# Filter steps, in-place sums and small stores moved in the first phase of a long convolution with a gate; ScalarE's long jobs of the last phase put into separate rows

## The chip, the cores and the metric

The kernel runs on one core of a Trainium2 chip. The metric is the device time of one execution in microseconds. TensorE is the matrix engine (PE in the profile), VectorE is DVE, ScalarE is ACT, GpSimd is POOL, and SyncE (SP) only issues transfers. Three of the engines issue transfers in this kernel: SyncE, ScalarE and GpSimd, each from its own queue, in which a transfer stands among the engine's other work and waits in line.

## The reference, cut to what matters

All arrays are float32 on entry, batch 4, sequence 12800, width 128.

```python
h_mlp = np.maximum(pos_emb @ w1, 0.0) @ w2          # the filter, made from pos_emb
h_filt = h_mlp * np.exp(-0.01 * pos)[:, None]
u = x * v
y = irfft(rfft(u, n=2*S) * rfft(h_filt, n=2*S)[None], n=2*S)[:, :S]
x = x * y                                            # the long convolution, gated by x
gate_pre[t] = sum over k < 5 of conv_w[k] * x[t - 4 + k]
out = (sigmoid(gate_pre) * (x @ w_val)) @ w_out
```

## The kernel before, in words

The sequence of 12800 is cut into J = 2 halves of 6400, and each half into N1 = 100 by N2 = 64. The transforms are matrix products over n1 (100) and n2 (64).

**First phase** (`signal` and `filt`). For each of the 64 n2 a tile of x and v is loaded by three transfers on SyncE (64, 32 and 4 partitions, L298). VectorE forms the product x*v in the tile's first half (`product`, L315). Two n2 form a pair, n2 and its mirror: `prep` forms their sum and difference in the tiles' second halves (L326, L327), and from these, for each n2, two sums us and ud (L334) in tiles of their own, two buffers each. TensorE multiplies us and ud with the table fsd into fp (L379, two matmuls for each of c = 0, 1), ScalarE copies fp to st (L380, two copies to one n2), and the spectrum part st is stored to the scratch tensor a_u in three transfers: 64 and 32 partitions from ScalarE's queue (L386), 4 partitions from SyncE's queue one n2 later (`flush`, L397). st has four buffers. The tiles for x and v come from a ring: four general buffers ld 0 to 3 and two own ones xv6, xv7, and from the time when the filter's input is used up also ld 4 and 5 (until the 48th load). A pair of tiles goes back to the ring after the second n2's us and ud are formed (`release`), and the next loads into them are issued there (`fetch`).

The filter is made beside it, in three parts that share the engines with the signal: 32 steps that transpose pos_emb and apply w1 (L228 to L242), 32 steps of the transform over n1 (L256 to L262, copied out by ScalarE), and 26 steps (one to begin with and 25 of four k1 each) of twiddle and transform over n2 (`turned`, L269 to L282: four ScalarE and four VectorE operations, eight matmul passes and a ScalarE copy). The two are written as generators. A list of costs gives each filter step a price, and after each half of an n2 as many filter steps are recorded as keep the spent cost in step with the signal's progress; the factor FS = 0.87 makes the filter end at about n2 = 56. By that list the three parts take 18.4, 20.7 and 16.5 n2. The order in which the code records the operations is the order of each engine's queue (`manual_schedule`); no scheduler moves anything there.

Six tables (dft, tw, inv and the three int64 weight arrays) are loaded from ScalarE's queue at n2 = 8 and 12. Near the end GpSimd issues the first loads of the second phase (rows of a_u that are complete); the rest of these rows come from SyncE.

**Second phase** (`filter_pair`, `spectrum`, `times`, `inverse`): pairs of k1, not touched.

**Last phase** (from L547): 32 groups of R = 4 rows; every row passes through y_sum (TensorE, sd), y_copy (ScalarE, sd_sb L602), y_trans two rows later (TensorE transposes tp L609, ScalarE dif L611), y_join (VectorE yr L619 and L620, GpSimd product into ext L622), five taps of the short convolution for a whole group (tap 0 on ScalarE, gt L634; taps 1 to 4 on VectorE, one in each row, L637), a sigmoid for a whole group (ScalarE, sg L641), the value product (TensorE, v_ps L646), the gated product (VectorE, gd L651), the projection (TensorE, o_ps L656) and a copy and store (ScalarE, o_sb L664). ext holds 16 rows and 4 rows of halo in front; every fourth group begins a new ext, and `fill_halo` copies the last four rows of the one before (L588), or parts of the tail rows at the start of a half (L583 to L586), and for the last ext of a half also the tail rows (L590). In the loop, tap 0 of the next group, the sigmoid and the halo copy all stand in row 3 of the four. In what follows rows are counted r = 0 to 3 as in the loop, and a row's operations stand in each engine's queue in the order in which the loop writes them.

Of the kernel before, what the change touches and what calls it, by code (L numbers as in the profile page):

```python
# [9 lines left out]
F32 = mybir.dt.float32  # L10
# [13 lines left out]
B, S, D, FO, KC = 4, 12800, 128, 64, 5  # L24
J, N1, N2 = 2, 100, 64
# [4 lines left out]
R = 4  # L30
# [88 lines left out]
def tile_longconv_gate(  # L119
# [20 lines left out]
    nc = tc.nc  # L140
# [41 lines left out]
    BD = B * D  # L182
# [23 lines left out]
    with tc.tile_pool(name="p1", bufs=1) as p1, tc.tile_pool(name="ps1", bufs=1, space=PSUM) as ps1:  # L206
# [77 lines left out]
                yield  # L284

        ring = list(enumerate(LD[0:4]))
        ring += [(6, p1.tile([128, 4 * BD], F32, name="xv6")), (7, p1.tile([128, 4 * BD], F32, name="xv7"))]
        for i, (_, t) in enumerate(ring):
            (nc.vector, nc.gpsimd)[i in (2, 5)].memset(t, 0.0)
        ahead, fetched = [], [0]  # L290
        BACK = 48

# [8 lines left out]
                    free_at[i] = n - 2 * N2  # L301
                fetched[0] += 1

        def release():
            for i, t, _ in pair:
                if i not in (4, 5) or fetched[0] < BACK:
                    ring.append((i, t))
            pair.clear()

        def halves(t):  # L310
            return t.rearrange("p (w h e) -> p w h e", w=2, h=2)

# [2 lines left out]
            nc.vector.tensor_tensor(u[:, 0], u[:, 0], u[:, 1], op=ALU.mult)  # L315
            pair.append((*it, u))

        pair = []

        def prep(n):  # L320
            if n == 0:
                product(ahead.pop(0))
            if n % 2 == 0:
                product(ahead.pop(0))
                a, b = (u for _, _, u in pair)
                nc.vector.tensor_tensor(a[:, 1], a[:, 0], b[:, 0], op=ALU.add)  # L326
                nc.vector.tensor_tensor(b[:, 1], a[:, 0], b[:, 0], op=ALU.subtract)  # L327
                srcs = a, b
            else:
                srcs = pair[1][2], pair[0][2]  # L330
            out = []
            for c, op in enumerate((ALU.add, ALU.subtract)):
                w = p1.tile([128, BD], F32, name="us" if c == 0 else "ud", bufs=US)
                nc.vector.tensor_tensor(w, srcs[c][:, 1, 0], srcs[c][:, 1, 1], op=op)  # L334
                out.append(w)
            if n % 2 == 1:
                release()
                fetch()
                if n + 1 < N2:
                    product(ahead.pop(0))  # L340
            return out

        US = 2

        def signal():
            fetch(4)
            load_pos(0)
            fetch()
            load_pos(HC)
            ready = [prep(0)]  # L350
            for n in range(N2):
                if n == 8:
                    nc.scalar.dma_start(out=dft, in_=t_dft)
                    nc.scalar.dma_start(out=tw, in_=t_tw)
                    nc.scalar.dma_start(out=inv, in_=t_inv)
                if n == 12:
                    for dst, src in ((wval, w_val), (wout, w_out), (cw, conv_w.rearrange("k d -> d k"))):
                        raw = p1.tile(list(dst.shape), mybir.dt.int64, name=f"raw{len(raws)}")
                        nc.scalar.dma_start(out=raw, in_=src)
                        raws.append((dst, raw))  # L360
                if n in (18, 22, 26):
                    _narrow(nc, p1, *raws[n // 4 - 4])
                if n == BACK + 2:
                    load_w(0)
                if n == N2 - 3:
                    for part in EARLY:
                        load_a(0, part, nc.gpsimd)
                if n == N2 - 1:
                    for part in EARLY:
                        load_a(1, part, nc.gpsimd)  # L370
                if n + 1 < N2:
                    ready.append(prep(n + 1))
                both = ready.pop(0)
                st = p1.tile([128, 2, J * BD], F32, name="st", bufs=4)
                for c in range(2):
                    fp = ps1.tile([128, J, BD], F32, name="fp", bufs=2)
                    for j in range(J):
                        h = slice(j * 64, j * 64 + 64)
                        nc.tensor.matmul(out=fp[:, j], lhsT=fsd[h, c], rhs=both[c][h], start=True, stop=True)  # L379
                    nc.scalar.copy(out=st[:, c], in_=fp.rearrange("k j e -> k (j e)"))  # L380
                    yield
                src = st.rearrange("k c e -> k (c e)")
                row = n % 2 * N2 + n // 2 * 2
                dst = a_u[:, row:row + 2].rearrange("k c e -> k (c e)")
                for k0, k, step, p0 in PARTS[:2]:
                    nc.scalar.dma_start(out=dst[k0:k0 + k], in_=src[p0:p0 + step * (k - 1) + 1:step])  # L386
                rest.append((dst, src))
                if len(rest) > 1 or n + 1 == N2:
                    flush()
# [3 lines left out]
        def flush():  # L393
            while len(rest) > 1 or rest and n_done[0]:
                dst, src = rest.pop(0)
                k0, k, step, p0 = PARTS[2]
                nc.sync.dma_start(out=dst[k0:k0 + k], in_=src[p0:p0 + step * (k - 1) + 1:step])  # L397

        n_done = [False]

        FS = 0.87
        with tc.manual_schedule():
            sig, fil = signal(), filt()
            n_sig = 2 * N2
            cost = [0.7, 0.9] * (J * N2 // 8) + [0.9] * (FO // 2) + [0.4] + [0.9] * (N1 // 4)
            spent, steps = 0.0, iter(cost)
            for i in range(n_sig):
                next(sig, None)
                while spent < sum(cost) and spent * n_sig * FS <= (i + 1) * sum(cost):
                    next(fil, None)  # L410
                    spent += next(steps, sum(cost))
            for _ in sig:
                pass
            n_done[0] = True
            flush()
            for _ in fil:
                pass
# [126 lines left out]
    with tc.tile_pool(name="p3", bufs=1) as p3, tc.tile_pool(name="ps3", bufs=1, space=PSUM) as ps3:  # L544
# [3 lines left out]
        EG = 4  # L548
# [27 lines left out]
        def fill_halo(j, q):  # L576
            e = exts[j, q]
            if q == 0:
                t, m = tails[j], N1 // 2
                if j == 0:  # L580
                    nc.vector.memset(e[:, 0:HALO, :, 0:1], 0.0)
                else:
                    nc.scalar.copy(out=e[:, 0:HALO, :, 0:1], in_=tails[j - 1][:, :, :, m + 1:m + 2])  # L583
                nc.scalar.copy(out=e[:, 0:HALO, :, 1:m + 1], in_=t[:, :, :, 0:m])
                nc.scalar.copy(out=e[:, 0:HALO, :, m + 1:N1 - 1], in_=t[:, :, :, m + 2:N1])  # L585
                nc.scalar.copy(out=e[:, 0:HALO, :, N1 - 1:N1], in_=t[:, :, :, m:m + 1])  # L586
            else:
                nc.scalar.copy(out=e[:, 0:HALO], in_=exts[j, q - 1][:, EG * R:])  # L588
            if q == NG // EG - 1:
                nc.scalar.copy(out=e[:, EG * R:], in_=tails[j])  # L590

        def y_sum(s, r):
            sd = ps3.tile([128, B * D], F32, name="sd", bufs=2)
# [76 lines left out]


        AHEAD3, NT, LAG = 3, len(groups), 2
        y_run, gd_last, o_last = [], None, None
        with tc.manual_schedule():
            for s in range(3):
                load_rows(s, (2,))
# [5 lines left out]
            for t in range(-AHEAD3, NT + 2):  # L682
# [9 lines left out]
                for r in range(R):  # L692
                    done = y_run.pop(0) if len(y_run) == LAG or s >= NT and y_run else None
                    if done:
                        y_trans(*done)
                    v_ps = value(t - 1, r) if 0 <= t - 1 < NT else None
                    if o_last is not None:
                        finish(*o_last)
                        o_last = None
                    if gd_last is not None:  # L700
                        o_last = gd_last[0], gd_last[1], project(gd_last[2])
                        gd_last = None
                    if s < NT and r % 2 == 0:
                        y_sum(s, r)
                        y_sum(s, r + 1)
                    if 0 <= t < NT:
                        tap(t, r + 1)
                    if r == R - 1 and 0 <= t + 1 < NT:
                        tap(t + 1, 0)
                    if v_ps is not None:  # L710
                        gd_last = t - 1, r, gated(t - 1, r, v_ps)
                    if done:
                        y_join(*done)
                    if s < NT:
                        y_copy(s, r)
# [46 lines left out]
```

## Time and profile before

| | |
|---|---|
| median of 3 runs | 1182.41 us (1181.82 to 1184.42) |
| the profiled execution's own time | 1177.74 us, of which its span 1176.0 us |
| mean granted TensorE clock | 0.953 |
| busy over the span: TensorE, VectorE, ScalarE, GpSimd | 1027.8, 992.6, 622.6, 679.7 us |
| moved by DMA | 329.98 MB, mean 281 GB/s |
| stretch 340 to 380 us | end of the first phase; ScalarE's last copy into st at 378 us |
| stretch 400 to 760 us | second phase |
| stretch 811 to 1135 us | last phase, full rows |

In a row of the timeline stand the start and the length in us, the engine, the line, the operation with the tile that it writes and those that it reads, and in brackets how long the engine stood idle before it and on what. An engine's name with a q (ACTq, SPq) is its queue issuing a transfer. In the table of windows each engine's busy time stands with its count of instructions. Waits are inferred from semaphores: where several were waited for, the last one is named, and an engine that is kept at its own transfer issue is shown as waiting for some transfer.

### The profile page before, as it was taken

The numbers are of one execution on the slowest core, as the hardware profiler recorded it, in microseconds if no ns is written. First come the engines' busy times: TensorE is split into PE (matmuls) and PEld (weight loads), VectorE is DVE, ScalarE is ACT, GpSimd is POOL, SyncE is SP. The second block draws the span as 40 slices with busy tenths as digits, with TensorE's granted clock in tenths as the row PEclk, the third lists the DMA queues.
The fourth block names the chain that finished last, engine by engine and source line by source line (L and its number), as shares of the span: only waits on it lengthen the run. The fifth ranks groups of instructions, "written<-read, shape, count | busy, mean of one in ns | idle before, by whom it ended". The sixth has DMA issues, their size and how long they took to land. (4 is left out here: it accounts for less than half of the span.)

```text
span 1176.0 us, 19204 instructions
## 1 busy us (share of the span) xinstructions
PE 1027.8 (87%) x6968; PEld 479.7 (41%) x6968; DVE 992.6 (84%) x1146; ACT 622.6 (53%) x1000; POOL 679.7 (58%) x290
## 2 busy tenths in 40 slices
PE   3767788967675799999999999988999999999986
PEld 1333345534341344444444444333444444444432
DVE  6678886659986799999999999718999999999996
ACT  1233366667774244444444444346676767676763
POOL 1000000000000699999999999928889898898880
PEclk9789889888989799999999999999999999999999
DMA  8889898875879789989999989787787777687622
GB/s 253 289 312 321 287 336 323 310 254 203 307 277 323 260 300 307 311 305 311 309 311 310 314 307 306 245 284 291 272 304 260 282 276 295 263 312 259 236 85 112
DMA packets 81384, 329.98 MB, mean 281 GB/s; under 512 B 11812, under 2 KB 13036, under 8 KB 62092
## 3 DMA queue, kind: packets, MB, share of 16 engines
q1 hardware_dynamic: 38512, 196.90, 50.1%
q10 hardware_dynamic: 42204, 130.02, 28.0%
q0 software_dynamic: 576, 1.84, 0.6%
q8 instruction: 57, 0.93, 0.3%
q14 instruction: 35, 0.29, 0.1%
HBM read 197.64 MB, written 131.07 MB: 280 GB/s over the span
## 5 line engine op out<-in xcount | busy, mean ns | idle before, releaser
L622 POOL TENSOR_TENSOR ext<-yr,xr 128x400 f32<-128x400 f32 x120 | 303.2, 2528 | 40.5 <-DVE yr L620 38.3
L637 DVE SCALAR_TENSOR_TENSOR gt<-ext,cw,gt 128x1600 f32<-128x1600 f32 x128 | 240.7, 1881 | 0.8 <-ACT gt L634 0.8
L380 ACT COPY st<-fp 128x1024 f32<-128x1024 f32 x128 | 128.7, 1027 | 174.9 <-PE fp L379 66.7
L484 ACT COPY c_sb<-c_ps 128x1024 f32<-128x1024 f32 x100 | 101.4, 1014 | 201.7 <-PE c_ps L479 194.8
L479 PE MATMUL c_ps<-va,ld 64*64 64x512 f32 x1600 | 194.1, 594 | 0.0
L468 DVE TENSOR_TENSOR va<-z_ps,h_sb 128x2048 f32<-128x2048 f32 x50 | 114.6, 2291 | 49.7 <-ACT h_sb L452 32.9
L513 POOL TENSOR_TENSOR va<-va,vb 128x1024 f32<-128x1024 f32 x50 | 118.6, 2373 | 45.6 <-DVE vb L468 45.5
L198 POOL DMA_DIRECT2D ld<-a_u x4 | 2.7, 683 | 240.6 <-DMA a_u<-st 240.6
L379 PE MATMUL fp<-us,fsd 64*128 64x512 f32 x256 | 87.2, 763 | 62.3 <-ACT st L380 35.5
L656 PE MATMUL o_ps<-gd,wout 128*128 128x400 f32 x256 | 112.4, 521 | 19.2 <-DVE gd L651 11.2
L595 PE MATMUL sd<-ld,inv 128*64 128x512 f32 x512 | 124.8, 605 | 2.0 <-ACT sd_sb L602 1.0
L522 POOL TENSOR_TENSOR va<-va,vb 128x1024 f32<-128x1024 f32 x50 | 119.6, 2392 | 0.0
L521 POOL TENSOR_TENSOR vc<-vc,vd 128x1024 f32<-128x1024 f32 x50 | 119.0, 2379 | 0.0
L462 PE MATMUL z_ps<-ld,ld 64*64 64x512 f32 x800 | 111.3, 606 | 7.4 <-DMA a_u<-st 4.0
L479 PEld LDWEIGHTS c_ps<-va,ld 64*64 64x64 f32 x1600 | 73.7, 135 | 101.2 <-issue 100.9
L602 ACT COPY sd_sb<-sd 128x512 f32<-128x512 f32 x128 | 76.1, 595 | 72.2 <-PE sd L595 55.5
L468 DVE TENSOR_TENSOR vb<-z_ps,h_sb 128x2048 f32<-128x2048 f32 x50 | 114.0, 2280 | 0.0
L646 PE MATMUL v_ps<-ext,wval 128*128 128x400 f32 x256 | 107.1, 500 | 0.0
L479 PE MATMUL c_ps<-vc,ld 64*64 64x512 f32 x800 | 98.2, 604 | 3.6 <-ACT c_sb L484 3.6
L609 PEld LDWEIGHTS tp<-ident,sd_sb 128*128 128x128 f32 x512 | 58.3, 140 | 75.8 <-PE sd L595 49.5
L609 PE MATMUL tp<-ident,sd_sb 128*128 128x128 f32 x512 | 79.9, 280 | 3.7 <-DVE yr L620 2.6
L619 DVE TENSOR_TENSOR yr<-tp,dif 128x204 f32<-128x204 f32 x128 | 45.9, 358 | 42.0 <-ACT dif L611 40.8
(85 smaller groups left out, 1560.6 us busy)
## 6 DMA issues: line engine op xcount, KB each, us to landing
c_y<-c_sb ACTq DMA_DIRECT2D x100, 512.0 KB
ld<-a_u SPq DMA_DIRECT2D x48, 1024.0 KB
a_u<-st ACTq DMA_DIRECT2D x64, 512.0 KB
ld<-c_y SPq DMA_DIRECT2D x64, 512.0 KB
xr<-in_xt_dram SPq DMA_DIRECT2D x32, 800.0 KB
out_dram<-o_sb ACTq DMA_DIRECT2D x32, 800.0 KB
ld<-in_xv_dram SPq DMA_DIRECT2D x46, 512.0 KB
a_u<-st ACTq DMA_DIRECT2D x64, 256.0 KB
```

The costliest lines, as they stand in the source:

```text
L380: nc.scalar.copy(out=st[:, c], in_=fp.rearrange("k j e -> k (j e)"))
L462: nc.tensor.matmul(out=z[half[h], c], lhsT=wk[half[c], 0, half[h]], rhs=a2[half[c], h, j], start=True, stop=True)
L468: nc.vector.tensor_tensor(out, z.rearrange("p (b d) -> p b d", d=D).unsqueeze(1).to_broadcast([128, n, B, D]), h_sb.unsqueeze(2).to_broadc ...
L479: nc.tensor.matmul(out=c_ps[half[m], h], lhsT=wk[half[h], 1 + c, half[m]], rhs=vt[half[h], c].rearrange("p b d -> p (b d)"), start=(i == 0 ...
L513: nc.gpsimd.tensor_tensor(va[:, 0:2], va[:, 0:2], vb[:, 0:2], op=ALU.add)
L521: nc.gpsimd.tensor_tensor(vc, vc, vd, op=ALU.add)
L522: nc.gpsimd.tensor_tensor(va[:, 2:4], va[:, 2:4], vb[:, 2:4], op=ALU.add)
L595: nc.tensor.matmul(out=sd[c * N2:(c + 1) * N2], lhsT=inv[:, c], rhs=rows_in[s, c][:, r * B * D:(r + 1) * B * D], start=True, stop=True)
L609: nc.tensor.transpose(out=tp[:, b], in_=t[:, b], identity=ident)
L622: nc.gpsimd.tensor_tensor(e[:, r0 + r], yr, xr, op=ALU.mult)
L637: nc.vector.scalar_tensor_tensor(gt, rows(t, k), cw[:, k:k + 1], gt, op0=ALU.mult, op1=ALU.add)
L656: nc.tensor.matmul(out=o_ps, lhsT=wout, rhs=gd, start=True, stop=True)
```

## The change: what it does

In the first phase:

- us and ud lose their tiles. The sums are written into the first half of the pair's tiles, whose products are no longer needed then. A tile of x and v is therefore given back later: after the second n2's matmuls instead of after its sums.
- The ring has one tile more (xv8): seven, and nine when ld 4 and 5 join it.
- The list of costs is gone. The filter's parts are spread evenly over n2 = 2 to 17 (32 steps), 17 to 35 (32) and 35 to 62 (26).
- The 4-partition stores of st and the six table loads are issued from GpSimd instead of SyncE and ScalarE; one more of the starting memsets is GpSimd's.

In the last phase the halo copy moves from row 3 to row 0 of the next group, tap 0 of the next group from row 3 to row 1, the copy of the tail rows to row 2; the sigmoid stays in row 3.

SyncE's queue in the first phase before; ld_74 to ld_77 are ring tiles, the L397 rows the small stores of st, two n2 each time:

```order
L397 DMA a_u<-st 4x2048 x2
L298 DMA ld_74<-in_xv_dram 64x2048
L298 DMA ld_74<-in_xv_dram 32x2048
L298 DMA ld_74<-in_xv_dram 4x2048
L298 DMA ld_75<-in_xv_dram 64x2048
L298 DMA ld_75<-in_xv_dram 32x2048
L298 DMA ld_75<-in_xv_dram 4x2048
L397 DMA a_u<-st 4x2048 x2
```

and GpSimd's queue now, from the last starting memset's successor on (a_u<-st are the same small stores, raw the int64 weights, ld_78 and ld_79 the filter's input buffers, cleared before they join the ring):

```order
L398 DMA a_u<-st 4x2048 x7
L352 DMA dft<-in_tab_dft_dram 128x256
L353 DMA tw<-in_tab_tw_dram 128x200
L354 DMA inv<-in_tab_inv_dram 128x128
L398 DMA a_u<-st 4x2048 x4
L358 DMA raw_523<-in_moe_w_val_dram 128x128
L358 DMA raw_525<-in_moe_w_out_dram 128x128
L358 DMA raw_527<-in_moe_conv_w_dram 128x5x1
L398 DMA a_u<-st 4x2048 x5
L248 MEMSET ld_78 128x2048
L248 MEMSET ld_79 128x2048
L398 DMA a_u<-st 4x2048 x44
```

The small stores stand no longer between the loads on SyncE, but behind each other on GpSimd, with the tables and two memsets between them.

ScalarE's queue in the last phase before, at the row in which a new ext has begun (dif, o_sb and sd_sb are each row's own copies):

```order
L611 COPY dif<-tp_6325 128x204
L664 COPY o_sb<-o_ps 128x400
L634 ACTIVATE gt<-ext,cw 128x1600
L602 COPY sd_sb<-sd 128x512
L641 ACTIVATE sg<-gt 128x1600
L588 COPY ext<-ext 128x1600
L611 COPY dif<-tp_6359 128x204
L664 COPY o_sb<-o_ps 128x400
L602 COPY sd_sb<-sd 128x512
```

and now, from the halo copy of row 0 to row 3's first copies:

```order
L587 COPY ext<-ext 128x1600
L608 COPY dif<-tp_6260 128x204
L661 COPY o_sb<-o_ps 128x400
L664 DMA out_dram<-o_sb 128x1600
L599 COPY sd_sb<-sd 128x512
L631 ACTIVATE gt<-ext,cw 128x1600
L608 COPY dif<-tp_6284 128x204
L661 COPY o_sb<-o_ps 128x400
L599 COPY sd_sb<-sd 128x512
L608 COPY dif<-tp_6312 128x204
L661 COPY o_sb<-o_ps 128x400
L599 COPY sd_sb<-sd 128x512
```

The three operations of 128x1600 stood between one sd_sb's two neighbours; now the row's three copies stand between any two of them, and the sigmoid follows the last row shown.

The diff, without the lines that only delete or rename what is named above:

```diff
         ring += [(6, p1.tile([128, 4 * BD], F32, name="xv6")), (7, p1.tile([128, 4 * BD], F32, name="xv7")),
+                 (8, p1.tile([128, 4 * BD], F32, name="xv8"))]
         for i, (_, t) in enumerate(ring):
-            (nc.vector, nc.gpsimd)[i in (2, 5)].memset(t, 0.0)
+            (nc.vector, nc.gpsimd)[i in (2, 4, 6)].memset(t, 0.0)
...
-                w = p1.tile([128, BD], F32, name="us" if c == 0 else "ud", bufs=US)
+                w = srcs[c][:, 0, n % 2]
                 nc.vector.tensor_tensor(w, srcs[c][:, 1, 0], srcs[c][:, 1, 1], op=op)
                 out.append(w)
             if n % 2 == 1:
-                release()
-                fetch()
+                using.append(list(pair))
+                pair.clear()
...
+        def release():
+            for i, t, _ in using.pop(0):
+                if i not in (4, 5) or fetched[0] < BACK:
+                    ring.append((i, t))
+            fetch()
...
-                    nc.scalar.dma_start(out=dft, in_=t_dft)
+                    nc.gpsimd.dma_start(out=dft, in_=t_dft)
...
                 for k0, k, step, p0 in PARTS[:2]:
                     nc.scalar.dma_start(out=dst[k0:k0 + k], in_=src[p0:p0 + step * (k - 1) + 1:step])
+                if n % 2 == 1:
+                    release()
...
-                nc.sync.dma_start(out=dst[k0:k0 + k], in_=src[p0:p0 + step * (k - 1) + 1:step])
+                nc.gpsimd.dma_start(out=dst[k0:k0 + k], in_=src[p0:p0 + step * (k - 1) + 1:step])
...
-        FS = 0.87
+        spans = [(J * N2 // 4, 15), (FO // 2, 18), (N1 // 4 + 1, 27)]
+        due = [2 + sum(w for _, w in spans[:k]) + w * i / n for k, (n, w) in enumerate(spans) for i in range(n)]
...
-            for i in range(n_sig):
+            for i in range(2 * N2):
                 next(sig, None)
-                while spent < sum(cost) and spent * n_sig * FS <= (i + 1) * sum(cost):
+                while due and due[0] <= i / 2:
                     next(fil, None)
-                    spent += next(steps, sum(cost))
+                    due.pop(0)
...
-                    if r == R - 1 and 0 <= t + 1 < NT:
-                        tap(t + 1, 0)
...
+                    if r == 0 and halo:
+                        fill_halo(*halo)
+                    if r == 1 and 0 <= t + 1 < NT:
+                        tap(t + 1, 0)
+                    if r == 2 and halo:
+                        if halo[1] == NG // EG - 1:
+                            nc.scalar.copy(out=exts[halo][:, EG * R:], in_=tails[halo[0]])
+                        halo = None
                     if r == R - 1 and 0 <= t < NT:
                         sigmoid(t)
-                    if r == R - 1 and s < NT and g % EG == 0:
-                        fill_halo(j, g // EG)
+                if s < NT and g % EG == 0:
+                    halo = j, g // EG
```

More of the change, by code (lines that the diff above doesn't have):

```diff
@@ L286, in tile_longconv_gate @@
         ring = list(enumerate(LD[0:4]))
-        ring += [(6, p1.tile([128, 4 * BD], F32, name="xv6")), (7, p1.tile([128, 4 * BD], F32, name="xv7"))]
+        ring += [(6, p1.tile([128, 4 * BD], F32, name="xv6")), (7, p1.tile([128, 4 * BD], F32, name="xv7")),
+                 (8, p1.tile([128, 4 * BD], F32, name="xv8"))]
         for i, (_, t) in enumerate(ring):
-            (nc.vector, nc.gpsimd)[i in (2, 5)].memset(t, 0.0)
+            (nc.vector, nc.gpsimd)[i in (2, 4, 6)].memset(t, 0.0)
         ahead, fetched = [], [0]
@@ L302, in fetch @@
                 fetched[0] += 1
[L304 to L308, printed above, removed]
         def halves(t):
@@ L316, in product @@
             pair.append((*it, u))
-        pair = []
+        pair, using = [], []
         def prep(n):
@@ L341, in prep @@
             return out
-        US = 2
+        def release():
[3 more added lines that the diff above has]
+            fetch()
         def signal():
@@ L352, in signal @@
                 if n == 8:
-                    nc.scalar.dma_start(out=dft, in_=t_dft)
-                    nc.scalar.dma_start(out=tw, in_=t_tw)
-                    nc.scalar.dma_start(out=inv, in_=t_inv)
+                    nc.gpsimd.dma_start(out=dft, in_=t_dft)
+                    nc.gpsimd.dma_start(out=tw, in_=t_tw)
+                    nc.gpsimd.dma_start(out=inv, in_=t_inv)
                 if n == 12:
@@ L358, in signal @@
                         raw = p1.tile(list(dst.shape), mybir.dt.int64, name=f"raw{len(raws)}")
-                        nc.scalar.dma_start(out=raw, in_=src)
+                        nc.gpsimd.dma_start(out=raw, in_=src)
                         raws.append((dst, raw))
@@ L396, in flush @@
                 k0, k, step, p0 = PARTS[2]
-                nc.sync.dma_start(out=dst[k0:k0 + k], in_=src[p0:p0 + step * (k - 1) + 1:step])
+                nc.gpsimd.dma_start(out=dst[k0:k0 + k], in_=src[p0:p0 + step * (k - 1) + 1:step])
         n_done = [False]
-        FS = 0.87
+        spans = [(J * N2 // 4, 15), (FO // 2, 18), (N1 // 4 + 1, 27)]
+        due = [2 + sum(w for _, w in spans[:k]) + w * i / n for k, (n, w) in enumerate(spans) for i in range(n)]
+        sig, fil = signal(), filt()
         with tc.manual_schedule():
[L403 to L406, printed above, removed]
-            for i in range(n_sig):
+            for i in range(2 * N2):
                 next(sig, None)
-                while spent < sum(cost) and spent * n_sig * FS <= (i + 1) * sum(cost):
+                while due and due[0] <= i / 2:
                     next(fil, None)
-                    spent += next(steps, sum(cost))
+                    due.pop(0)
             for _ in sig:
@@ L588, in fill_halo @@
                 nc.scalar.copy(out=e[:, 0:HALO], in_=exts[j, q - 1][:, EG * R:])
-            if q == NG // EG - 1:
-                nc.scalar.copy(out=e[:, EG * R:], in_=tails[j])
         def y_sum(s, r):
@@ L672, in tile_longconv_gate @@
         AHEAD3, NT, LAG = 3, len(groups), 2
-        y_run, gd_last, o_last = [], None, None
+        y_run, gd_last, o_last, halo = [], None, None, None
         with tc.manual_schedule():
```

## The prediction, made before the changed kernel was run

> **What bounds the kernel now.** I read the busy windows of the stages first, then the waits, then the timeline of single queues. In the windows the columns are the length, the busy time of TensorE, its weight loads, VectorE, ScalarE and GpSimd, the granted clock, the DMA share and GB/s.
>
> ```profile
> 52.00:163.10 111.10, 84.89 (x431) 43.56 (x430) 90.15 (x130) 44.97 (x46) 3.61 (x2) 0.85 0.87 307
> 163.10:240.90 77.80, 69.08 (x490) 41.09 (x488) 56.69 (x74) 49.41 (x53) 0.00 (x0) 0.93 0.86 317
> 240.90:340.80 99.90, 71.33 (x325) 40.13 (x325) 80.74 (x158) 71.35 (x152) 0.00 (x0) 0.85 0.68 252
> 340.80:378.20 37.40, 23.36 (x92) 8.31 (x92) 29.47 (x36) 19.48 (x24) 2.73 (x4) 0.95 0.92 323
> 811.00:1135.00 324.00, 315.33 (x1328) 144.71 (x1328) 313.88 (x444) 227.98 (x396) 289.14 (x112) 1.00 0.70 265
> ```
>
> The change leaves the middle phase alone. The last one (the last row) keeps VectorE busy for 313.88 of 324.00 us, so 10.1 us are open there. In the first phase (the four rows above) no engine is full; its DMA runs at a share of 0.87, falls to 0.68 in the third row and ends at 0.92. The same windows over ScalarE's copy into st alone give the pace, two copies to one n2:
>
> ```profile
> 52.00:163.10 111.10, 37.86 (x38) 0.85 0.87 307
> 163.10:240.90 77.80, 31.06 (x30) 0.93 0.86 317
> 240.90:340.80 99.90, 32.31 (x32) 0.85 0.68 252
> 340.80:378.20 37.40, 17.56 (x18) 0.95 0.92 323
> ```
>
> So 19 n2 at 5.85 us, 15 at 5.19, 16 at 6.24 and 9 at 4.16: 326.2 us for 59 n2, 5.53 each. The slow third row is the filter's last part (n2 38 to 53); when it is done, the stores catch up at 4.16. Two bounds lie close together there. ScalarE's busy time per n2 is 3.29, 4.46 and 2.16 us in the last three rows; the rest of the pace is 1.90, 1.78 and 2.00, nearly constant, as it would be if ScalarE's queue, with its two store issues per n2, set the pace. The issues themselves are told by the timeline of ScalarE's and SyncE's queues:
>
> ```profile
> 197.47 1.11 ACTq L386 DMA_DIRECT2D a_u<-st  x2
> 199.79 4.49 SPq L397 DMA_DIRECT2D a_u<-st  x2
> 202.04 3.43 ACTq L386 DMA_DIRECT2D a_u<-st  x2
> 205.56 1.01 ACT L380 COPY st<-fp 128x1024 f32<-128x1024 f32 x1 [2.79 <-DMA a_u<-st]
> ```
>
> A pair of store issues costs 1.11 us when nothing stands in its way and 3.43 here, just after SyncE's two small ones took 4.49; ScalarE's next copy waits behind it.
>
> **The change part by part.** *Last phase.* One group of four rows out of 16 puts three long jobs behind each other on ScalarE:
>
> ```profile
> 875.49 1.64 ACT L634 ACTIVATE gt<-ext,cw 128x1600 f32<-128x1600 f32 x1
> ...
> 877.49 1.56 ACT L641 ACTIVATE sg<-gt 128x1600 f32<-128x1600 f32 x1
> 878.93 1.53 ACT L588 COPY ext<-ext 128x1600 f32<-128x1600 f32 x1
> 880.35 0.35 ACT L611 COPY dif<-tp 128x204 f32<-128x204 f32 x1
> 880.79 0.37 DVE L619 TENSOR_TENSOR yr<-tp,dif 128x204 f32<-128x204 f32 x1 [0.99 <-ACT dif L611]
> ...
> DVE yr L619 <- ACT dif L611: 10.1, 7, 2.4
> ```
>
> The last row, the waits of VectorE from 811 to 1135, says that these seven places are all its idle time: 10.1 us. Now each row of four has at most one long job. Does it fit? A row lasts 852.04 - 849.22 = 2.82 us on VectorE, and dif is ready well ahead of its reader:
>
> ```profile
> 847.84 0.59 ACT L602 COPY sd_sb<-sd 128x512 f32<-128x512 f32 x1 [0.41 <-ACT o_sb L664]
> ...
> 848.44 0.33 ACT L611 COPY dif<-tp 128x204 f32<-128x204 f32 x1
> 849.22 1.87 DVE L637 SCALAR_TENSOR_TENSOR gt<-ext,cw,gt 128x1600 f32<-128x1600 f32 x1
> 850.87 0.59 ACT L602 COPY sd_sb<-sd 128x512 f32<-128x512 f32 x1 [1.71 <-PE sd L595]
> 851.50 0.36 DVE L619 TENSOR_TENSOR yr<-tp,dif 128x204 f32<-128x204 f32 x1
> 852.04 1.87 DVE L637 SCALAR_TENSOR_TENSOR gt<-ext,cw,gt 128x1600 f32<-128x1600 f32 x1
> 852.30 0.33 ACT L611 COPY dif<-tp 128x204 f32<-128x204 f32 x1 [0.85 <-PE tp L609]
> 854.32 0.36 DVE L619 TENSOR_TENSOR yr<-tp,dif 128x204 f32<-128x204 f32 x1
> ```
>
> The slack is 1.69 us (852.63 to 854.32) in odd rows and 2.73 (848.77 to 851.50) in even ones. Row 0's halo copy of 1.53 starts behind its sd_sb, at 851.46, and ends at 852.99: row 1's dif starts 0.7 late. In odd rows the next dif follows sd_sb at once (847.84 + 0.59 to 848.44), so row 1's first tap of 1.64 makes row 2's dif as much late, 2.3 with the 0.7 before it, against 2.73; the sigmoid in row 3 delays the next row's by 1.56. Nothing is late on VectorE, the dearest case by 0.4. Bounds: 0 (each job still shifts a yr) and -10.1; I take -10, since all three margins hold.
>
> *First phase, filter steps.* They move from crowded to even: 32 steps over 15 n2, 32 over 18, 26 over 27 (the last stand in the 16 of the third row now). No step is removed, so ScalarE's and VectorE's sums stay. If the evened pace is that of the 163 to 241 row, 5.19, which carries filter work too, 59 n2 take 306.2 us: -20. If n2 4 to 22 keep their 5.85, since their work gets no lighter (the first part gets 15 n2 where the old cost list gave it 18.4), only 40 n2 go to 5.19: 207.6 for 215.1, -7.5. If ScalarE's queue is the bound, its 49.41 + 71.35 + 19.48 = 140.24 us of work in these 40 n2 (3.51 each) plus 1.90 is 5.41 wherever the steps stand: 0. I take -13, between the first two, because the third row's DMA share of 0.68 is room, and VectorE's 257 us of 326 (its column's sum) leave it too.
>
> *Sums in place, more tiles, later release.* This takes away VectorE's waits for us and ud, and makes loads wait for TensorE instead of VectorE:
>
> ```profile
> DVE ud L334 <- PE fp L379: 19.5, 14, 2.6
> ...
> DVE us L334 <- PE fp L379: 9.4, 7, 1.8
> ...
> DVE ld L315 <- DMA ld<-in_xv_dram: 1.5, 1, 1.5
> ```
>
> The 28.9 us are waits for an engine that lags, not of the pace, and loads made VectorE wait 1.5 us in all: neither edit has a price of its own; both are cover for the -13. A tile held two n2 longer (11 us at 5.53) against one tile more (5.5 us) leaves the loads 5.5 us less ahead. Without cover that is a wait for loads, queued on SyncE with the filter's loads behind it.
>
> *Small stores and tables from GpSimd.* SyncE sheds 64 issues, ScalarE six. Behind the stores on GpSimd stand two memsets and the first loads of the middle phase. The trace has four issues from there, and the last small store of SyncE with the load that waited for it:
>
> ```profile
> L198 POOL DMA_DIRECT2D ld<-a_u x4: 639/642/808, 351.6 to 366.0; - x4
> DMA to landing us min/median/max: 5.8/9.0/12.0
> 350.00:360.00 10.00, 4.17 (x16) 1.64 (x16) 9.93 (x12) 3.85 (x4) 1.45 (x2) 0.90 1.00 320
> 381.20 0.50 SPq L397 DMA_DIRECT2D a_u<-st  x1
> 383.73 2.43 SPq L198 DMA_DIRECT2D ld<-a_u  x6
> ```
>
> 64 issues of 0.64 us are 41 us on an engine with nothing else to do. A tile of st comes round every fourth n2 (22 us); copies 2, issue 0.64 and a landing of at most 12.0 (for 448 KB) fit. Only the end shows it: the load at 383.73 came 2.5 us after that store's issue; from GpSimd it is between 2.6 (an issue 0.14 longer) and 5.8 (the shortest landing there), so +0.1 to +3.3; I take +1, as 32 KB lie nearer to the first. The six table issues gone from ScalarE are in the -13.
>
> [...]
>
> **Sum.** -13 - 10 + 1 = -22. The profiled execution took 1177.74 us (span 1176.0 and 1.7 around it), so 1155.7; it lay 4.67 under the median of the runs shown, 1182.41, so I forecast **1160 us**, own range 1152 to 1168.
>
> **Rivals.** *A: the first phase gives nothing* (ScalarE's queue or the DMA is full in its sense already). For it: the near constant 1.78 to 2.00 us above. Against it: the first row's 3.48 (5.85 less 44.97/19), which is no such constant. -10 + 1: 1173.
>
> *B: the DMA evens out as well.* The four rows moved 34.1 + 24.7 + 25.2 + 12.1 = 96.0 MB; at the 323 GB/s of the last one, all of it takes 297 us, -29, and with the last phase -38: 1144. For it: a share of 0.87 in the first rows beside 0.92. Against it: the last row is mostly stores. [...]
>
> *C: slower, by ScalarE's store issues.* Loads are now released by the matmul that ScalarE's copy waits for too, so SyncE's burst of six and that row's two stores are taken in together. One of two issues is slow already (3.43 beside 1.11). If the other one becomes slow as well, 2.32 us per pair of n2, 1.16 per n2, over 40 n2 it is +46, with the last phase +37: 1219. It decides once phase one loses 11.4 (so that 2.4 are left after the last phase's -10 and the +1), 0.29 per n2: when a quarter of the quick issues turn slow. Against it: the bursts stay one per two n2, with two issues less between them.
>
> **How the numbers follow.** The measurement tells about 0.2% (2.4 us) from no change. Forecast 0.47; A 0.24; B 0.15; C 0.09; that phase one loses just what the last one gains, 0.05. Faster: 0.47 + 0.24 + 0.15 - 0.02 (A's upper end) = 0.84; same 0.07; slower 0.09. The range takes in A's far side and B's near one: 1143 to 1177; about 0.07 lies below, 0.13 above.
>
> **What would show it.** Last phase: VectorE's waits for dif gone, 314 us where 324 stood. First phase: share of 0.85 or more throughout, pace of 5.2 to 5.4 without a 6.2 and a 4.2, store issues on ScalarE mostly of 1.1 us, the middle phase starting some 12 us earlier, at 388 for 400. Wrong: pace unchanged (A), DMA above 0.9 (B), ScalarE's issues over 2 us each time (C), or VectorE waiting for xv.

## Result and profile after

| | before | after |
|---|---|---|
| median | 1183.41 us (1181.82 to 1185.98, 4 runs) | 1137.99 us (1135.12 to 1141.04, 4 runs) |
| ratio to before | | 0.9615, 95% interval 0.9582 to 0.9647 |
| profiled execution, its span | 1177.74, 1176.0 us | 1139.08, 1137.3 us |
| mean granted clock | 0.953 | 0.955 |

The change makes the kernel 45 us faster, twice the 22 of the forecast (1160), and lands below the range of 1143 to 1177. An interval of 0.003 to 0.004 on a ratio is 4 to 5 us here, so differences between two versions of less than that are told only where they come back.

The copies of ScalarE into st in the kernel after, in windows whose edges are the second copies of n2 = 4, 23, 38, 53 and 63 (columns: length, ScalarE's busy time in these copies, clock, DMA share, GB/s):

```profile
49.06:158.73 109.67, 38.85 (x38) 0.86 0.86 303
158.73:230.00 71.27, 31.09 (x31) 0.98 0.95 345
230.00:307.03 77.03, 29.54 (x31) 0.87 0.87 321
307.03:352.79 45.76, 20.13 (x21) 0.85 0.82 280
```

That is 5.77, 4.75, 5.14 and 4.58 us per n2, where 5.85, 5.19, 6.24 and 4.16 stood (there the third row had 16 n2 and the fourth 9). The 6.2 and the 4.2 are evened out, as forecast, but the second row is faster than the 5.19 that the forecast took for the best, and its DMA share is 0.95 for 0.86. The queue that loads x and v looks different too, at first sight. SyncE, before:

```profile
155.08 5.95 SPq L298 DMA_DIRECT2D xv<-in_xv_dram  x6
161.12 1.13 SPq L397 DMA_DIRECT2D a_u<-st  x2
163.84 4.56 SPq L298 DMA_DIRECT2D ld<-in_xv_dram  x6
170.35 1.42 SPq L397 DMA_DIRECT2D a_u<-st  x2
174.28 3.93 SPq L298 DMA_DIRECT2D ld<-in_xv_dram  x6
```

and after:

```profile
150.39 1.70 SPq L299 DMA_DIRECT2D xv<-in_xv_dram  x3
152.14 27.63 SPq L299 DMA_DIRECT2D ld<-in_xv_dram  x18
179.97 11.10 SPq L299 DMA_DIRECT2D xv<-in_xv_dram  x9
```

The bursts of six loads with pauses have become one row, but only because nothing else of SyncE stands between the loads any more; the pauses lie inside that row. The line itself (shortest, middle and longest issue in ns, first and last start) and SyncE's waits from 150 to 230 us (us in all, times, longest) tell it:

```profile
L299 SPq DMA_DIRECT2D ld<-in_xv_dram x18: 469/526/1192, 152.1 to 179.2; - x18
SPq L299 <- PE fp L378: 23.3, 8, 4.1
```

An issue takes about 0.5 us. SyncE waited 23.3 us for matmuls that give tiles back, as the prediction said that the loads would, and, by the same view, 26 us for earlier transfers. The end of the first phase after (the last copies, the last small store, the load that waits for it, TensorE's next phase):

```profile
351.83 1.93 ACT L379 COPY st<-fp 128x1024 f32<-128x1024 f32 x2 [1.31 <-PE fp L378]
354.05 0.58 POOL L398 DMA_DIRECT2D a_u<-st  x1 [2.62 <-ACT st L379]
358.32 4.17 SPq L198 DMA_DIRECT2D ld<-a_u  x7
361.24 4.55 PE L461 MATMUL z_ps<-ld,ld 64*64 64x512 f32 x14 [6.76 <-DMA ld<-a_u]
```

and before:

```profile
378.28 1.93 ACT L380 COPY st<-fp 128x1024 f32<-128x1024 f32 x2 [1.41 <-PE fp L379]
384.92 4.21 PE L462 MATMUL z_ps<-ld,ld 64*64 64x512 f32 x14 [3.99 <-DMA a_u<-st]
```

From the end of the last copy to TensorE it is 361.24 - 353.76 = 7.5 us for 4.7, 2.8 longer. The last phase, after, in the windows of all engines (TensorE, weight loads, VectorE, ScalarE, GpSimd, clock, share, GB/s):

```profile
770.00:1100.00 330.00, 326.90 (x1390) 151.40 (x1389) 330.00 (x467) 243.52 (x419) 305.95 (x118) 0.99 0.72 273
```

VectorE is busy for all of 330 us, where it had 313.88 of 324. TensorE begins the last phase's y_sum here, before and after:

```profile
776.64 1.94 PE L595 MATMUL sd<-ld,inv 128*64 128x512 f32 x8
750.46 2.44 PE L592 MATMUL sd<-ld,inv 128*64 128x512 f32 x8 [1.64 <-DMA ld<-c_y]
```

From the two traces: the first phase's last copy ends 26.4 us earlier, the middle phase starts 23.7 earlier, the last phase 26.2, and the end comes 38.7 earlier. So some 12 us are the last phase, and the middle phase makes up for the 2.8 us at its start. How much of the first phase's 26 belongs to which edit, the two traces cannot tell.

### The profile page after: what moved, and what is told of

Same layout as the page of the kernel before. It is cut to its first block, busy times and chain, and to the rows that moved or that the text cites. A ratio compares the mean times of both kernels' runs of the same rounds, so it can differ in the third digit from the quotient of the medians.

```text
span 1137.3 us, 19288 instructions
## 1 busy us (share of the span) xinstructions
PE 1018.2 (90%) x6968; PEld 482.2 (42%) x6968; DVE 992.0 (87%) x1146; ACT 626.2 (55%) x1000; POOL 723.2 (64%) x361
## 4 chain that ended last, share of the span: by engine, by line
PE 35%; DVE 23%; issue 10%; ACT 5%; DMA 3%; ACTq 1%; SPq 0%; DVEq 0%
PE c_ps L478 22%; DVE gt L634 11%; PE z_ps L461 8%; DVE gd L648 6%; DVE yr L616 3%; ACT st L379 3%; DVE yr L617 2%; PE c_ps L445 2%; ACTq L385 1%; ACT fk L269 1%; DMA c_y<-c_sb 1%; DMA a_u<-st 1%; PE fp L378 1%; PE sd L592 1%; DMA ld<-c_y 0%
## 5 line engine op out<-in xcount | busy, mean ns | idle before, releaser
L398 POOL DMA_DIRECT2D a_u<-st x64 | 36.4, 569 | 297.8 <-ACT st L379 242.5
L378 PE MATMUL fp<-ld,fsd 64*128 64x512 f32 x320 | 99.5, 718 | 49.9 <-DVE ld L329 16.9
L606 PEld LDWEIGHTS tp<-ident,sd_sb 128*128 128x128 f32 x512 | 58.3, 141 | 75.3 <-PE sd L592 49.7
L648 DVE TENSOR_TENSOR gd<-v_ps,sg 128x400 f32<-128x400 f32 x128 | 71.2, 556 | 3.1 <-PE v_ps L643 1.9
```

What stands on the lines that cost most here:

```text
L606: nc.tensor.transpose(out=tp[:, b], in_=t[:, b], identity=ident)
L648: nc.vector.tensor_tensor(gd, v_ps, gate_sg[t][:, r * ROW:(r + 1) * ROW], op=ALU.mult)
```

## Experiments

In what follows "the changed kernel" is the one after (1137.99), and each kernel is timed beside the kernel before (whose medians were 1180.99 to 1183.41 there); n2 stands for one step of the first phase. The table gives medians and the ratio to before; the text goes by them, and for the DMA by the window of 160 to 230 us, where the filter is mostly in its second part and the granted clock is 0.94 to 0.99 in the rows shown. The expectations number the theories of why the first phase gained more than forecast: 1, the small stores stood in SyncE's queue between the loads and held them up; 2, four-row transfers from SyncE and ScalarE lower the rate of the DMA, whatever they stand between; 3, the sums in place free VectorE; 4, the even filter pace; 5, the number of transfers issued from SyncE and ScalarE. The kernel before has in the window:

```profile
160.00:230.00 70.00, 61.89 (x440) 37.19 (x440) 51.64 (x69) 45.43 (x49) 0.00 (x0) 0.94 0.87 320
```

and the changed kernel:

```profile
160.00:230.00 70.00, 64.14 (x460) 39.09 (x459) 51.44 (x79) 52.61 (x65) 8.47 (x15) 0.98 0.95 344
```

| kernel | median us | ratio (95%) |
|---|---|---|
| before + last phase (a_last) | 1170.87 | 0.9904 (0.9865 to 0.9942) |
| before + small stores (i_small_only) | 1163.56 | 0.9834 (0.9795 to 0.9874) |
| before + sums in place (k_sums_only) | 1176.16 | 0.9938 (0.9917 to 0.9959) |
| before + filter pace (j_pace_only) | 1173.83 | 0.9911 (0.9877 to 0.9945) |
| before + table loads (q_tables_only) | 1184.28 | 1.0011 (0.9978 to 1.0044) |
| after, small stores on SyncE (c_small_sync) | 1153.01 | 0.9747 (0.9714 to 0.9780) |
| after, the same one n2 later (m_sync_later) | 1161.66 | 0.9833 (0.9815 to 0.9851) |
| after, small stores on ScalarE (g_small_act) | 1160.13 | 0.9821 (0.9793 to 0.9848) |
| after, small stores on SyncE, small loads on GpSimd (l_swap) | 1135.83 | 0.9617 (0.9586 to 0.9648) |
| after, small loads on GpSimd too (h_pool_loads) | 1132.52 | 0.9587 (0.9558 to 0.9615) |
| after, loads 16 + 16 rows (n_split_even) | 1141.10 | 0.9643 (0.9610 to 0.9676) |
| after, loads 24 + 8 rows (p_split_uneven) | 1150.44 | 0.9727 (0.9695 to 0.9760) |
| after, old filter pace (d_oldpace) | 1135.15 | 0.9590 (0.9548 to 0.9633) |
| after, sums in own tiles (e_sums_apart) | 1144.71 | 0.9679 (0.9656 to 0.9702) |
| h_pool_loads with a pace of 19, 19, 22 (o_h_pace) | 1132.70 | 0.9556 (0.9511 to 0.9601) |
| h_pool_loads with the old pace (r_h_oldpace) | 1133.15 | 0.9561 (0.9513 to 0.9608) |
| after, once more (s_after_again) | 1139.78 | 0.9647 (0.9609 to 0.9686) |
| h_pool_loads, once more (t_loads_again) | 1133.96 | 0.9598 (0.9559 to 0.9638) |

**The last phase alone.** The kernel before with the diff's last hunks (`fill_halo`, tap 0, the tail's copy and the halo in rows of their own).

```diff
-                    if r == R - 1 and 0 <= t + 1 < NT:
-                        tap(t + 1, 0)
+                    if r == 0 and halo:
+                        fill_halo(*halo)
+                    if r == 1 and 0 <= t + 1 < NT:
+                        tap(t + 1, 0)
...
```

> The kernel before with the change to the last phase alone. The first phase is then as before (middle phase starting at about 400 us, 50 of the 52 slices of pace unchanged at 5.85, 5.19, 6.24 and 4.16 us per n2). If the -10 of the prediction's last-phase term stands by itself: 10 to 12 us under the kernel before, VectorE's waits for dif gone and VectorE busy in all of the stretch of 324 us. If the last phase gained only because the earlier phases changed: 0 to 3 us.

11.7 us faster (1170.87 for 1182.52). VectorE's waits for dif from 745 us to the end, before (columns: us in all, times, longest):

```profile
DVE yr L619 <- ACT dif L611: 40.8, 14, 21.0
```

and in this kernel:

```profile
DVE yr L617 <- ACT dif L609: 30.0, 6, 20.9
...
805.00:1130.00 325.00, 321.39 (x1370) 149.34 (x1371) 325.00 (x459) 240.92 (x413) 300.62 (x117) 1.00 0.73 275
```

10.8 us of waits are gone, the long first one stays, and VectorE has no idle time left. The gain does not hang on the first phase. This kernel's first phase is that of before, and its last copy into st starts at 384.8, where before's profiled execution had 379.2: that execution lay under its median by about what its first phase was short.

**Small stores back on SyncE.**

```diff
-                nc.gpsimd.dma_start(out=dst[k0:k0 + k], in_=src[p0:p0 + step * (k - 1) + 1:step])
+                nc.sync.dma_start(out=dst[k0:k0 + k], in_=src[p0:p0 + step * (k - 1) + 1:step])
```

> The changed kernel with the 64 four-row stores back on SyncE's queue. Theory 1 (the stores stood in SyncE's queue between loads and held up the tiles of st or the loads): at least 10 us slower than the changed kernel, the pace of n2 38 to 63 back from 4.91 to 5.2 or more, ScalarE's store issues again up to 3.4 us. [...] Theory 3 (sums in place free VectorE from TensorE) and theory 4 (the even filter pace): 0 to 3 us slower. All theories: the first phase's end 2 to 3 us shorter, since the last small store is again SyncE's (4.7 us from the last copy to TensorE's z where the changed kernel has 7.5).

15 us slower than the changed kernel, although the phase's end is shorter (2.2 us from the last copy to TensorE for 7.5). So this one line, which the prediction gave no price but +1 at the end, carries a third of the gain or more. Its window and SyncE's queue:

```profile
160.00:230.00 70.00, 63.10 (x462) 39.10 (x461) 47.91 (x71) 50.38 (x59) 0.00 (x0) 0.98 0.92 328
...
157.69 1.12 SPq L398 DMA_DIRECT2D a_u<-st  x2
161.42 5.84 SPq L299 DMA_DIRECT2D ld<-in_xv_dram  x6
167.36 1.70 SPq L398 DMA_DIRECT2D a_u<-st  x2
172.03 3.70 SPq L299 DMA_DIRECT2D ld<-in_xv_dram  x6
```

The stores stand between SyncE's bursts of loads again (theory 1 has that as the cause), and the DMA share and rate are lower again (theory 2). This kernel fits both.

**The old filter pace.** `spans` and `due` out, the cost list with FS = 0.87 in.

```diff
-                while due and due[0] <= i / 2:
+                while spent < sum(cost) and spent * n_sig * FS <= (i + 1) * sum(cost):
                     next(fil, None)
...
```

> The changed kernel with the filter's steps at the old places (crowded to the front and into n2 38 to 53). Theory 4 (the even pace is what gave n2 38 to 63 their 14.5 us): 12 to 15 us slower than the changed kernel, the DMA share in n2 38 to 53 back to about 0.7 and the pace there to 6.2, then 4.2. Theories 1 and 2 (small stores): the DMA catches up before and after the crowded part, so 3 us or less. Theory 3 (sums in place): VectorE's lead covers the crowded part, 3 us or less.

1135.15 for 1137.99: theory 4 falls, undoing the even pace costs nothing. The windows of the copies into st, edges at the first copies of n2 = 4, 23, 38, 53 and 63:

```profile
49.70:150.46 100.76, 38.58 (x38) 0.90 0.94 332
150.46:218.25 67.79, 31.71 (x31) 1.00 0.98 366
218.25:310.50 92.25, 30.33 (x31) 0.83 0.73 261
310.50:351.56 41.06, 19.59 (x20) 0.88 0.90 310
```

5.30, 4.52, 6.15 and 4.11 per n2: the crowded stretch costs 15 us against the changed kernel (92.25 for 77.03), and the other three give back 17; the filter's first two parts are spread over more n2 here (18.4 and 20.7 for 15 and 18) and its last part ends sooner. Note the second row: 366 GB/s at a share of 0.98, with the four-row loads still on SyncE.

**Sums in tiles of their own**, two of each, eight tiles for x and v, given back at once.

```diff
-                w = srcs[c][:, 0, n % 2]
+                w = p1.tile([128, BD], F32, name="us" if c == 0 else "ud", bufs=2)
...
```

> The changed kernel with the sums in tiles of their own again (two of each), eight tiles for x and v instead of nine, and tiles let go at once after the sums. Theory 3 (with the sums in place VectorE no longer waits for TensorE, and its lead evens out the rest): 10 us or more slower than the changed kernel, VectorE's waits for us and ud back with 25 us or more. Theories 1, 2 and 4: 0 to 4 us slower; the waits of VectorE may come back, but they are waits for an engine that lags.

6.7 us slower, between the bounds set for it. VectorE's waits for ud and us are 7.8 and 3.3 us here, not the 25 expected. Theory 3 is a smaller part, not the cause.

**Small stores on SyncE, small loads on GpSimd.** The test between the two theories that were left: SyncE's order of stores and loads is as with the stores back on SyncE, and the bytes that leave in four-row transfers from SyncE and ScalarE are as many as in the changed kernel, so by theory 2 the 15 us come back.

```diff
-                    nc.sync.dma_start(out=t[p0:p0 + step * (k - 1) + 1:step], in_=xv[n, k0:k0 + k])
+                    (nc.gpsimd if k0 == 96 else nc.sync).dma_start(out=t[p0:p0 + step * (k - 1) + 1:step], in_=xv[n, k0:k0 + k])
...
```

> The changed kernel with the four-row stores back on SyncE, and in their place the four-row loads of x and v from GpSimd: as many bytes in four-row pieces leave SyncE's and ScalarE's queues as in the changed kernel, only other ones. [...] Theory 1 (a store that waits for ScalarE's copy stands in SyncE's queue ahead of loads that could go): nothing in that order has changed, 10 to 15 us slower than the changed kernel.

1135.83, all of it back, with the stores still between the loads on SyncE. The window:

```profile
160.00:230.00 70.00, 62.27 (x452) 37.79 (x452) 50.65 (x78) 50.59 (x64) 7.86 (x14) 0.99 0.95 339
```

Theory 1 falls; share and rate are close to those of the changed kernel (0.95 and 344).

**Small stores on SyncE, one n2 later.**

```diff
-            while len(rest) > 1 or rest and n_done[0]:
+            while len(rest) > 2 or rest and n_done[0]:
...
```

> The changed kernel with the four-row stores back on SyncE, each put one n2 later in the program (5 us), so that the copy that it waits for is long done when SyncE comes to it. Theory 1 (the store's wait in SyncE's queue holds loads up): most of the 15 us come back, at most 5 us slower than the changed kernel. [...]

23.7 us slower than the changed kernel, where theory 1 allowed 5: nothing comes back, and it is 9 us slower than with the stores on SyncE at their old place. ScalarE's waits for st from 45 to 350 us:

```profile
ACT st L379 <- PE fp L378: 58.9, 36, 7.2
ACT st L379 <- DMA a_u<-st: 58.3, 19, 6.5
```

58.3 us for stores, where the kernel with the stores on SyncE at their old place has the first of these lines and the changed kernel the second:

```profile
ACT st L379 <- DMA a_u<-st: 28.6, 7, 7.2
ACT st L379 <- DMA a_u<-st: 2.3, 1, 2.3
```

Tiles of st held longer are the likely reason for the 9.

**Small stores on ScalarE.**

```diff
-                nc.gpsimd.dma_start(out=dst[k0:k0 + k], in_=src[p0:p0 + step * (k - 1) + 1:step])
+                nc.scalar.dma_start(out=dst[k0:k0 + k], in_=src[p0:p0 + step * (k - 1) + 1:step])
```

> The changed kernel with the four-row stores on ScalarE's queue, behind ScalarE's own two. [...] Theory 1 (stores held loads up in SyncE's queue): SyncE is free of them here too, so only ScalarE's issues cost: 64 of 0.55 us are 35 us of a queue that is 57% busy, 0 to 7 us slower.

22 us slower, with SyncE's queue free of stores:

```profile
160.00:230.00 70.00, 60.50 (x445) 36.43 (x445) 45.17 (x65) 44.56 (x52) 0.00 (x0) 0.98 0.90 315
```

As theory 2 has it; the 7 us beyond the 15 of the stores on SyncE are what ScalarE's own issues may cost, which was not separated.

**Small loads on GpSimd as well.** The edit of the loads above, with the stores left on GpSimd.

> The changed kernel with the four-row loads of x and v from GpSimd as well as the four-row stores. [...] Theory 1 (stores held loads up in SyncE's queue): SyncE's queue is already free of waits on stores, so within 3 us; slower if a load that waits for its tile on GpSimd holds up the stores behind it.

5.5 us faster than the changed kernel, beyond the 3 that theory 1 allowed, with a share of 0.98:

```profile
160.00:230.00 70.00, 62.08 (x440) 38.19 (x440) 54.64 (x73) 53.65 (x73) 18.15 (x32) 0.97 0.98 364
```

**Loads of 32 rows cut in two.** 16 and 16 rows, or 24 and 8, each from SyncE: 64 issues more, as many as the change took away.

```diff
                 for k0, k, step, p0 in PARTS:
-                    nc.sync.dma_start(out=t[p0:p0 + step * (k - 1) + 1:step], in_=xv[n, k0:k0 + k])
+                    for a, m in ((0, 24), (24, 8)) if k == 32 else ((0, k),):
+                        q0 = p0 + step * a
+                        nc.sync.dma_start(out=t[q0:q0 + step * (m - 1) + 1:step], in_=xv[n, k0 + a:k0 + a + m])
```

> [...] Theory 5 (what counts is the number of transfers issued from SyncE and ScalarE, not where their rows land): the 15 us that 64 such issues cost come back as a loss, 10 to 18 us slower than the changed kernel. [...]

> [...] Theory 5 (number of issues): the same as with 16 and 16, within 3 us.

16 and 16: 3.1 us slower than the changed kernel, which is not clear of noise, the window at the changed kernel's share and rate:

```profile
160.00:230.00 70.00, 62.22 (x454) 38.17 (x456) 50.88 (x77) 53.04 (x67) 8.46 (x15) 0.99 0.95 342
```

24 and 8: 9.3 us slower than 16 and 16, with the same issues and bytes, and 335 GB/s in the window for 342. So it is not the number of issues (theory 5 falls), but how the rows divide between the transfers.

**The edits of the first phase one by one, on the kernel before.** Small stores alone:

> The kernel before with its 64 four-row stores from GpSimd and nothing else changed. [...] If it needs the sums in place (tiles asked for earlier) to be of use: 0 to 5 us.

19.7 us faster (1163.56 for 1183.31), without the sums in place and somewhat more than the 15.0 that undoing it costs in the changed kernel, and share and rate go up with nothing else changed:

```profile
160.00:230.00 70.00, 66.79 (x484) 40.29 (x484) 53.85 (x73) 49.10 (x51) 8.24 (x15) 0.95 0.94 340
```

Sums in place, nine tiles and the later release alone (the diff's hunks of `ring`, `prep` and `release`):

> The kernel before with the sums in place, nine tiles for x and v and their later release, nothing else changed. If the 6.7 us that this part was worth in the changed kernel are a gain of its own (VectorE no longer waits for us and ud, SyncE asks for loads earlier): 4 to 9 us faster than the kernel before. [...]

7.2 us faster by the medians; its share in the window stays at 0.87. Pace alone (the reverse of the edit of the old pace):

> The kernel before with the filter's steps at their new places and nothing else changed. The prediction's step (evened pace by itself is worth -13, bounds -20 to 0): 7 to 20 us faster than the kernel before. [...]

7.9 us faster by the medians, at the low end of the 7 to 20 expected. The copies into st in windows from the second copies of n2 = 4, 23, 38 and 53 to that of 63:

```profile
51.85:169.22 117.37, 38.45 (x39) 0.85 0.86 301
169.22:246.09 76.87, 31.13 (x31) 0.91 0.85 311
246.09:329.31 83.22, 29.64 (x32) 0.82 0.80 296
329.31:379.13 49.82, 20.13 (x21) 0.93 0.76 263
```

6.18, 5.12, 5.55 and 4.98 per n2: the crowded stretch is gone, but no row comes under 4.9, and the four take 327.3 us where before's profiled execution, some 5 us under its median, had 326.2. Tables alone:

> The kernel before with its six table loads from GpSimd instead of ScalarE and nothing else changed. Six issues of 0.5 to 2.3 us less in ScalarE's queue in n2 8 to 12, and 0.6 MB of small transfers: 0 to 3 us faster. The small stores, the sums and the last phase alone give -19.7, -7.2 and -11.6 of the -45.4, so 7 us are open for this, the pace and what they do together.

Nothing; in the trace of before the six issues had taken 0.35 to 0.59 us each. Alone, the edits give -11.7, -19.7, -7.2, -7.9 and nothing for the tables: -46.5 where all together give -45.4. That is close, but they do not simply add: taken out of the changed kernel the pace is worth nothing, the small stores 15.0, the sums 6.7.

**Other paces with the small loads on GpSimd.** The small loads on GpSimd, and the filter spread over 19, 19 and 22 n2, or by the old cost list:

```diff
-        spans = [(J * N2 // 4, 15), (FO // 2, 18), (N1 // 4 + 1, 27)]
+        spans = [(J * N2 // 4, 19), (FO // 2, 19), (N1 // 4 + 1, 22)]
```

> The changed kernel with the four-row loads from GpSimd too and the filter spread over 19, 19 and 22 n2 in place of 15, 18 and 27. The loads alone gave 5.5 us. [...] If the DMA is the bound all through (its share 0.98 from 160 to 230 us), the pace gives nothing: 4 to 7 us faster, as with the loads alone.

> The changed kernel with the four-row loads from GpSimd too and the filter's steps at the old places. If the pace is worth nothing anywhere (as with the changed kernel, where the old places were 3 us faster within the uncertainty): 4 to 9 us faster than the changed kernel. [...]

1132.70 and 1133.15, as with the loads alone (1132.52): three paces, one time. The changed kernel and the loads once more, side by side on one chip:

> The changed kernel itself, on the same chip and in the same rounds as the version with the four-row loads from GpSimd, since their intervals against the kernel before (0.9582 to 0.9647 and 0.9558 to 0.9615) overlap. Expected from the earlier runs: 1135 to 1140 us.

> The changed kernel with the four-row loads of x and v from GpSimd too, beside the changed kernel itself. [...]

1139.78 (1135.51 to 1146.08) and 1133.96 (1130.15 to 1138.42): 5.8 us, after 5.5 the first time. The single times overlap, but both comparisons have one sign and nearly one size: the version with all four-row transfers from GpSimd is the fastest found, 0.9598 of before (0.9559 to 0.9638).

## Why the prediction was wrong

**The last-phase term was right.** -10 was forecast, 11.7 measured alone, from the waits that the prediction named.

**The step that failed is "Small stores and tables from GpSimd"**, which gave the stores no price but +1 at the end. So the term stood in the sum as +1; alone it is worth -19.7 us, and undone in the changed kernel it costs 15.0. The step asked what a small store costs the engine that issues it and who waits behind it; it did not ask whether the DMA keeps its rate when another engine issues the store. What the runs show, in the window from 160 to 230 us: the DMA moves less with the four-row stores issued from SyncE or ScalarE than with the same ones from GpSimd (320 GB/s before and 340 with them alone moved; 344 in the changed kernel, 328 with them back on SyncE, 315 with them on ScalarE), and most with the four-row loads from GpSimd too (364). It does not matter whether the four-row loads or the four-row stores are moved (1135.83 and 1137.99), nor, within the noise, how often transfers are issued (1141.10 with 64 more). The loss comes back on either of the two other queues (1153.01 on SyncE, 1160.13 on ScalarE). A 32-row load cut unevenly costs 9.3 us more than one cut evenly. By their rates in the same window the kernels fall into three groups: 309 to 328 GB/s in seven where small loads and small stores leave from SyncE or ScalarE, 339 to 346 in the seven with whole 32-row loads or even halves where one of the two leaves from GpSimd, 360 to 364 in the four where both do. Whether GpSimd's queue also helps as a third one beside the two was not tried apart from this; the uneven cut shows that the division of the rows counts without it.

**Why the issuer counts was not shown.** That the issuer and the division of the rows count is shown by these runs; what makes them count is not, since the trace gives only the mean over 16 engines. Nor did the mean share stop at one value: the window from 160 to 230 us has 0.87 in the kernel before and 0.95 in the changed one, but also 0.92 with the stores back on SyncE, and the second row of the old pace has 0.98 at 366 GB/s, with the four-row loads on SyncE. Why stays open.

**The filter's -13 was too much, and its bounds were not what held.** Alone the pace gives 7.9. That is near the bound of -7.5, but not by its case, in which n2 4 to 22 keep 5.85 and the other 40 go to 5.19: with the pace alone these took 6.18 and 5.25. The bound of -20 rested on "the evened pace is that of the 163 to 241 row, 5.19", and that row was no floor. With the small stores moved and the old pace kept (i_small_only), the same stretch, n2 23 to 38, takes 4.78 per n2:

```profile
162.40:234.10 71.70, 31.25 (x30) 0.95 0.94 344
```

In the changed kernel the crowded filter costs nothing in sum: with the old pace n2 38 to 53 fall back to 6.15, and the rows beside it make it good at 5.30, 4.52 and 4.11. In the kernel before, the rows ahead stayed at 5.85 and 5.19, and only the one behind came to 4.16. That the freer DMA is what lets them catch up, and not the sums and the larger ring, is an argument from these rows, not a run of its own.

**Sums in place were not mere cover.** "No price of its own" was forecast; they are worth 7.2 alone and 6.7 undone. VectorE's waits for us and ud are gone as forecast, but how the gain divides between them and the earlier loads of the larger ring was not tried.

**The end of the first phase** cost +2.8 in the traces, inside the bounds of +0.1 to +3.3, above the +1 taken; the middle phase makes up for it, and the last phase starts 26.2 us earlier, nearly the 26.4 of the last copy. The issue itself is cheap: the profile's group of the 64 small stores, busy time and mean ns of one, has

```profile
L398 POOL DMA_DIRECT2D a_u<-st x64 | 36.4, 569 | 297.8 <-ACT st L379 242.5
```

so one takes 569 ns, the longest 709, with VectorE busy for 272.33 of the 332.7 us in which they stand (22 to 354.7). With the stores on SyncE the end is 2.2 us; leaving only the last one there was not tried.

**Of the rivals,** A (first phase gives nothing) and C (ScalarE's issues turn slow) did not come. C's price came from a misread row: the 3.43 us of a pair of store issues are two issues of 0.46 us and a wait of 2.5 us between them (shortest, middle and longest issue in ns).

```profile
L386 ACTq DMA_DIRECT2D a_u<-st x2: 458/458/459, 202.0 to 205.0; - x2
```

B came nearest (1144 for 1137.99), with 0.15 for its chance. The signs by which the prediction would be told wrong named it: "DMA above 0.9". What spoke for B in the profile of before was there to be weighed: a share of 0.87 and 0.86 in two stretches with different work on the engines, beside 0.92 in the last row.

## What to carry to other kernels

In the kernel before the mean DMA share was 0.87 and 0.86 in two stretches with different work on the engines, and moving the four-row stores alone raised it from 0.87 to 0.94 in the window and gave 19.7 us. Where a share stays at one value below 1 in this way, look for transfers of few rows from SyncE or ScalarE, try them from GpSimd, and cut larger ones evenly (16 and 16 rows were 9.3 us faster than 24 and 8), before evening out compute. Test it by the rate in one window with the transfers moved and moved back (344 and 328 GB/s here); the share alone tells less (0.95 and 0.92). A moved transfer can have a price beyond what its issue costs and who waits behind it: the small stores take 569 ns each to issue from GpSimd, and back on SyncE they cost 15.0 us. A stretch's best pace before a change is a floor only if the resource that sets it stays as it is: 5.19 us per n2 became 4.78 with the small stores moved. In the timeline's row of a queue, the length divided by the count is not the time of one issue, since waits between the issues are in it (3.43 us for two issues of 0.46); the view of the single line tells them apart.

## What the runs showed of the hardware that was not expected

Four-row stores, 32 KB of the 800 KB stored per n2, cost 15 to 20 us of a first phase of some 350 to 380 when they leave from SyncE and not from GpSimd (1153.01 for 1137.99, 1183.31 for 1163.56). Moving the four-row loads in place of the stores gives the same (1135.83). A cut of 32 rows into 24 and 8 costs 9.3 us more than into 16 and 16 (1150.44 for 1141.10).
